# An mLSTM cell with a multiplicative FFN on one core: a chunk's own part of the outputs spread over all four quarters of TensorE

## The chip, the cores and the metric

The kernel runs on one core of one Trainium2 chip. The metric is the device time of one execution in microseconds (us). Executions of one kernel here differ by up to 4 us, and where that spread comes from is a part of the story. A "span" is the time from the first to the last instruction in the trace; it is about 1.8 us less than the device time.

## The reference

Two blocks, one after the other. The first is an mLSTM cell over 768 time steps for 4 batches of 8 heads of 40 dimensions; the second is an FFN without a nonlinearity on the 3072 tokens of 320 columns that the cell leaves. Cut to what matters:

```python
for t in range(S):
    m_new = np.maximum(f_gate[:, :, t] + m, i_gate[:, :, t])
    f_stab = np.exp(f_gate[:, :, t] + m - m_new)
    i_stab = np.exp(i_gate[:, :, t] - m_new)
    C = f_stab[..] * C + i_stab[..] * np.einsum('bhd,bhe->bhde', vt, kt)
    n = f_stab[..] * n + i_stab[..] * kt
    h_tilde = np.einsum('bhde,bhe->bhd', C, qt)
    denom = np.maximum(np.abs(nq), 1.0)
    y[:, :, t] = sigmoid(o_gate) * h_tilde / denom
...
a, b = x @ w1, x @ w2
return ((a * b) @ w3) @ w_out
```

## The kernel before

The kernel cuts time into blocks of 64 and works on two blocks of one batch at a time: a "chunk", 128 partitions, of which the lower and the upper half are the two blocks (`halves`). There are 24 chunks, numbered from 0, and one step for each. TensorE is used as four quarters of 64 rows by 64 columns: a product's row half is where its operands lie, its column half is where its output lies (`quarters`). In a full step TensorE does four groups of 16 small products, 32 instructions each, since the trace shows two for each f32 product:

- `ph`, the chunk's own part of the outputs: masked weights times values (`cell<-vbuf,pw` in the profile)
- `pi`, the part from the state before the block (`cell<-state,qT`)
- `ss`, the scores of the next chunk (`cell<-qT,kT`)
- `pc`, what the next chunk adds to the state (`cell<-vw,kbuf`)

Each step also has FFN work: the up projections (`pa`, `pb`), the down projection (`po`), early on the folding of w3 and w_out (`wp`), and late on a scheme of seven products in place of eight (`p`).

```python
halves = [slice(0, L), slice(L, P)]                 # L = 64, P = 128
quarters = ((0, 0), (1, 1), (0, 1), (1, 0))
...
ss, pc, pi = part(0, 0, L), part(0, NP * L, D1), part(1, 0, D1)
ph = [cell[1][halves[x], x, NP * D1:(NP + H) * D1]... for x in range(2)]
...
    for hd in range(H):                             # the own part: two quarters take turns
        for x, r in enumerate(halves):
            mm(ph[x][:, hd, :], pw[r, hd, :], vt[r, hd, :])
    for p in range(NP):                             # from the state: all four take turns
        for hip, x in quarters:
            mm(pi[halves[x], hip, p, :], qT[heads[hip], p, halves[x]], before[x][heads[hip], p, :])
...
# VectorE: h = pi * g, then h += ph, a half at a time
for x, r in enumerate(halves):
    nc.vector.tensor_tensor(out=h[r], in0=ph[x], in1=h[r], op=OP.add)
```

Of the kernel before, what the change touches and what calls it, by code (L numbers as in the profile page):

```python
# [11 lines left out]
OP = mybir.AluOpType  # L12
# [4 lines left out]
def kernel(  # L17
# [26 lines left out]
    nc = tc.nc  # L44

    B, H, S, D = q.shape
# [5 lines left out]
    NP = H // 2  # L52
    DP = 64
    D1 = D + 1
# [20 lines left out]
    cell = [ps_c.tile([P, 2, 512], FP, name=f"cell{i}", tag=f"cell{i}") for i in range(2)]  # L75
# [8 lines left out]
    def in_order(ins):  # L84

        if last:
            tc.add_manual_dep(ins.ins, last.pop().name, mybir.DependencyInfo(
                mybir.DependencyClass.NoSync, mybir.DependencyReason.DATA), reason="in_order")
        last.append(ins.ins)

    def mm(out, lhsT, rhs, start=True, stop=True):
        in_order(nc.tensor.matmul(out, lhsT=lhsT, rhs=rhs, start=start, stop=stop))  # L92
# [4 lines left out]
    halves = [slice(0, L), slice(L, P)]  # L97
    heads = [slice(0, D), slice(DP, DP + D)]
    quarters = ((0, 0), (1, 1), (0, 1), (1, 0))
# [207 lines left out]
    def decayed(new, old, n, x):  # L307
        c, b = divmod(n, B)
        nc.gpsimd.tensor_tensor(out=new, in0=old, op=OP.mult, in1=decay[:, b * NP:(b + 1) * NP, 2 * c + x:2 * c + x + 1]  # L309
                                .to_broadcast([P, NP, D1]))  # L310

    def quarter_work(s, rest):


        rest()

        def part(j, c0, n):
            return cell[j][:, :, c0:c0 + NP * n].rearrange("p x (n d) -> p x n d", d=n)

        ss, pc, pi = part(0, 0, L), part(0, NP * L, D1), part(1, 0, D1)  # L320
        ph = [cell[1][halves[x], x, NP * D1:(NP + H) * D1].rearrange("p (h d) -> p h d", d=D1) for x in range(2)]
        n = s - 1
        if 0 <= n < NU:
            pw, vt, qT = u_t.pop(n), vbuf[n % NB], qT_t.pop(n)
            before = before_t.pop(n)
            for hd in range(H):
                for x, r in enumerate(halves):
                    mm(ph[x][:, hd, :], pw[r, hd, :], vt[r, hd, :])
            for p in range(NP):
                for hip, x in quarters:  # L330
                    mm(pi[halves[x], hip, p, :], qT[heads[hip], p, halves[x]], before[x][heads[hip], p, :])
        n, first_read = s, None
        if n < NU:
            c, b = divmod(n, B)
            kt, vw = kbuf[n % NB], vw_t.pop(n)
            ends = range(2 if c < NT2 - 1 else 1)
            first, second, after = state[b]
            before_t[n] = first, second
            state[b] = after, second, first
            kT, qT, pw = kT_t.pop(n), qT_t[n], u_t[n]  # L340
            for p in range(NP):
                for hip, x in quarters:
                    mm(ss[halves[x], hip, p, :], kT[heads[hip], p, halves[x]], qT[heads[hip], p, halves[x]])
            for p in range(NP):
                for x, e in quarters:
                    if x in ends:
                        mm(pc[halves[e], x, p, :], kt[halves[x], 2 * p + e, :], vw[halves[x], 2 * p + e, :])
        den = None
        if 0 <= s - 1 < NU:
            den = outputs(s - 1, pi, ph)  # L350
        if n < NU:
            pv = pw.rearrange("p (n two) t -> p two n t", two=2)
            first_read = nc.vector.tensor_tensor(out=pv, in0=ss, in1=pv, op=OP.mult)
        with tc.issue_after(first_read.ins) if first_read else nullcontext():
            if n < NU:

                if c:
                    nc.vector.tensor_tensor(out=second, in0=pc[:, 0], in1=second, op=OP.add)
                else:
                    nc.vector.tensor_copy(out=second, in_=pc[:, 0])  # L360
                if len(ends) > 1:
                    decayed(after, second, n, 1)
            if den:
                done = den()
            if n < NU and len(ends) > 1:
                nc.vector.tensor_tensor(out=after, in0=pc[:, 1], in1=after, op=OP.add)
            if den:
                done = done()
        return done if den else first_read

    def outputs(n, pi, ph):
        c, b = divmod(n, B)
        hs = slice(b * H, (b + 1) * H)
        h = sb.tile([P, H, D1], FP, name="h", tag="h")
        nc.vector.tensor_tensor(out=h.rearrange("p (n two) d -> p two n d", two=2), in0=pi,
                                in1=gT[:, c, hs].rearrange("p (n two) -> p two n", two=2).unsqueeze(3)
                                .to_broadcast([P, 2, NP, D1]), op=OP.mult)
        for x, r in enumerate(halves):
            nc.vector.tensor_tensor(out=h[r], in0=ph[x], in1=h[r], op=OP.add)



        den = sb.tile([P, H, 1], FP, name="den", tag="den")

        def first():
            V = nc.vector
            V.tensor_scalar(out=den.bitcast(U32), in0=h[:, :, D:D1].bitcast(U32), scalar1=0x7FFFFFFF, scalar2=None,  # L387
                            op0=OP.bitwise_and)
            V.tensor_scalar(out=den, in0=den, scalar1=1.0, scalar2=2.0, op0=OP.max, op1=OP.mult)
            V.reciprocal(out=den, in_=den)  # L390
            return then

        def then():
            e = o_t.pop(n)
            nc.vector.scalar_tensor_tensor(out=e, in0=e, scalar=1.0, in1=den.to_broadcast([P, H, D]), op0=OP.add, op1=OP.mult)
            y_t[n] = sb.tile([P, DM + REM], FP, name="y", tag="y")
            return nc.vector.tensor_tensor(out=y_t[n][:, 0:DM].rearrange("p (h d) -> p h d", d=D), in0=h[:, :, 0:D],
                                           in1=e, op=OP.mult)

        return first  # L400
# [142 lines left out]
    for i, r in enumerate(third):  # L543
        nc.gpsimd.tensor_tensor(out=pick[r, :, i, :], in0=pair[r].to_broadcast([BH, B * NP, GC]), op=OP.mult,
                        in1=dec[r].unsqueeze(1).to_broadcast([BH, B * NP, GC]))
# [160 lines left out]
    for s in range(len(n_up)):  # L706
# [44 lines left out]
        def rest():  # L751
            for x in open_ups:
                up_rest(*x)
            if seven:
                seven[2]()

        gated = None
        if s <= NU:
            gated = quarter_work(s, rest)
        else:  # L760
            rest()
# [68 lines left out]
```

## Time and profile before

| | before |
|---|---|
| device time, median of 3 | 457.44 us (457.31 to 457.55) |
| TensorE busy | 434.4 us, 95% of the span |
| VectorE busy | 337.3 us, 74% |
| own part: products in a step | 32 instructions, from 208.19 to 208.99 us for 30 of them |
| additions of `ph` | 48 of 64x328, 497 ns each |

In the profile, PE is TensorE, PEld its weight loads, DVE VectorE, ACT ScalarE, POOL GpSimd. In a timeline a line has its start, its length, engine, line of code, operation, output and inputs, and how many instructions were merged. In the chain of waits a line has its start, its length and what took the time. A busy TensorE is not one at its peak here: by the profile products overlap (in the own part one lasts 227 ns in the median, and 30 start within 0.80 us), and a step in which it was busy throughout (15.87 us of 15.87) could still be shortened. The lines themselves stand in the prediction.

### The profile page before, as it was taken

The page shows a single profiled execution, that of the slowest core. Times are in us where ns is not written, and L with a number is a line of the kernel's source. Part 1 is how long each engine was busy: PE and PEld are TensorE (multiplying, and loading weights), DVE is VectorE, ACT ScalarE, POOL GpSimd, SP SyncE. Part 2 cuts the span into 40 slices and gives each one's busy share as a digit, 9 for nine tenths or more (in the row PEclk, how much of TensorE's full clock was granted, in tenths as well). Part 3 has the DMA queues.
Part 4 walks back from the last instruction along what each step waited for, and adds up shares of the span by engine and source line. Part 5 has one row for each costly group of instructions (what it writes and reads, how often), then busy time and mean ns, then how long its engine had stood idle before and what let it go on. Part 6 is the DMA issues. An engine that isn't in the chain of part 4 may idle for free.

```text
span 455.9 us, 12861 instructions
## 1 busy us (share of the span) xinstructions
PE 434.4 (95%) x5271; PEld 346.7 (76%) x5271; DVE 337.3 (74%) x655; ACT 134.4 (29%) x376; POOL 83.9 (18%) x156
## 2 busy tenths in 40 slices
PE   2986999999999999999999999999999999999997
PEld 2885878888778788887877877878778677777764
DVE  6689499989998988898867859659688756445530
ACT  3745355434443144133302320213210111001100
POOL 5343133233220221122022203202010000000000
PEclk9999799999999999999999999999999999999999
DMA  9989979788978788586356467274121110000001
GB/s 182 184 164 188 208 148 168 166 182 172 199 185 194 161 155 179 152 162 135 83 111 139 104 131 140 58 132 111 46 43 35 38 36 16 14 16 15 16 14 43
DMA packets 136554, 52.71 MB, mean 116 GB/s; under 512 B 109936, under 2 KB 127536, under 8 KB 136496
## 3 DMA queue, kind: packets, MB, share of 16 engines
q1 hardware_dynamic: 132896, 47.87, 52.4%
q10 hardware_dynamic: 3600, 4.03, 2.6%
q8 instruction: 41, 0.67, 0.7%
q14 instruction: 17, 0.14, 0.1%
HBM read 46.07 MB, written 5.80 MB: 114 GB/s over the span
## 4 chain that ended last, share of the span: by engine, by line
PE 80%; SPq 7%; DMA 5%; DVE 3%; issue 2%; POOL 1%; ACT 1%; DVEq 0%; ACTq 0%; POOLq 0%
PE cell L92 23%; PE pa L92 18%; PE po L92 13%; PE pb L92 11%; PE wp L92 8%; PE p L92 5%; SPq L173 3%; DMA kbuf<-in_k_dram 2%; SPq L128 1%; DMA q_all<-in_q_dram 1%; PE pt L95 1%; SPq L137 1%; PE px L95 1%; SPq L142 1%; DMA raw<-in_moe_w_out_dram 1%
## 5 line engine op out<-in xcount | busy, mean ns | idle before, releaser
L92 PE MATMUL po<-w3o,ab 128*128 128x320 f32 x224 | 62.2, 434 | 0.8 <-DVE ab L673 0.8
L92 PE MATMUL pa<-xT,w 128*128 128x256 f32 x240 | 62.2, 391 | 0.6 <-ACT xT L437 0.6
L92 PEld LDWEIGHTS po<-w3o,ab 128*128 128x128 f32 x224 | 42.3, 190 | 18.3 <-DVE ab L673 1.3
L309 POOL TENSOR_TENSOR state<-state,decay 128x164 f32<-128x164 f32 x40 | 19.8, 494 | 187.1 <-DVE den L387 161.8
L92 PEld LDWEIGHTS pa<-xT,w 128*128 128x128 f32 x240 | 45.7, 195 | 8.6 <-ACT xT L437 1.0
L630 DVE SCALAR_TENSOR_TENSOR a_sb<-pa,wo 128x512 f32<-128x512 f32 x12 | 8.3, 692 | 51.3 <-PE pa L92 51.3
L92 PE MATMUL pb<-xT,w 128*128 128x256 f32 x192 | 45.8, 382 | 0.0
L282 POOL TENSOR_SCALAR_AFFINE_SELECT pw<-pw 64x512 f32<-64x512 f32 x48 | 35.0, 728 | 54.3 <-ACT pw L280 52.8
L92 PE MATMUL cell<-w3o,ab 128*128 128x320 f32 x160 | 44.0, 432 | 0.0
L280 ACT ACTIVATE pw<-pw,aT 128x64 f32<-128x64 f32 x160 | 40.3, 336 | 2.9 <-ACT o_sb L685 2.4
L92 PEld LDWEIGHTS pb<-xT,w 128*128 128x128 f32 x192 | 37.0, 193 | 5.2
L92 PEld LDWEIGHTS cell<-w3o,ab 128*128 128x128 f32 x160 | 30.4, 190 | 12.0
L582 ACT ACTIVATE a_sb<-pa 128x512 f32<-128x512 f32 x24 | 14.3, 598 | 79.2 <-PE pb L92 79.2
L92 PE MATMUL pa<-xT,wr 64*64 64x256 f32 x384 | 36.8, 386 | 0.0
L92 PE MATMUL pb<-xT,wr 64*64 64x256 f32 x384 | 36.2, 379 | 0.0
L92 PE MATMUL wp<-wo,w3T 128*128 128x320 f32 x128 | 35.9, 433 | 0.2 <-DVE ab L583 0.2
L92 PEld LDWEIGHTS wp<-wo,w3T 128*128 128x128 f32 x128 | 23.7, 190 | 9.3 <-DVE ab L583 0.4
L92 PEld LDWEIGHTS pa<-xT,wr 64*64 64x64 f32 x384 | 19.0, 132 | 14.4 <-issue 8.4
L92 PEld LDWEIGHTS cell<-vbuf,pw 64*64 64x64 f32 x768 | 26.7, 138 | 4.2 <-issue 0.8
L583 DVE TENSOR_TENSOR ab<-pb,a_sb 128x512 f32<-128x512 f32 x24 | 16.4, 688 | 17.2 <-ACT a_sb L582 17.2
L92 PE MATMUL cell<-vbuf,pw 64*64 64x41 f32 x768 | 26.9, 229 | 0.0
L685 ACT COPY o_sb<-po 128x320 f32<-128x320 f32 x14 | 6.0, 426 | 68.9 <-PE po L92 68.9
(124 smaller groups left out, 761.6 us busy)
## 6 DMA issues: line engine op xcount, KB each, us to landing
raw<-in_moe_w_dram SPq DMA_DIRECT2D x64, 128.0 KB, 3.1
pw<-U_d SPq DMA_DIRECT2D x40, 128.0 KB, 3.9
kbuf<-in_k_dram SPq DMA_DIRECT2D x24, 160.0 KB, 4.6
vbuf<-in_v_dram SPq DMA_DIRECT2D x24, 160.0 KB, 4.9
o_in<-in_o_gate_dram SPq DMA_DIRECT2D x24, 160.0 KB, 4.4
out_dram<-o_sb ACTq DMA_DIRECT2D x24, 160.0 KB, 1.8
raw<-in_moe_w_dram SPq DMA_DIRECT2D x7, 512.0 KB, 5.9
raw<-in_moe_w_out_dram SPq DMA_DIRECT2D x32, 80.0 KB, 2.3
```

Of the source, the lines that this page charges most:

```text
L92: in_order(nc.tensor.matmul(out, lhsT=lhsT, rhs=rhs, start=start, stop=stop))
L95: in_order(nc.tensor.transpose(out, in_, ident[0:n, 0:n]))
L128: nc.sync.dma_start(out=dst, in_=rows(src, n))
L137: nc.sync.dma_start(out=dst[p0:p0 + 32, c0:c0 + NP * RAW].rearrange("r (p e) -> r p e", p=NP), in_=of.rearrange("p (r f) d -> r p (f d)", ...
L173: nc.sync.dma_start(out=dst, in_=src)
L280: nc.scalar.activation(out=pw[:, h, :], in_=src[:, h, :], func=AF.Exp, bias=aT[:, c, b * H + h:b * H + h + 1])
L282: nc.gpsimd.affine_select(out=pw[r], in_=pw[r], compare_op=OP.is_ge, fill=0.0, base=0, pattern=[[0, H], [1, L]], channel_multiplier=-1)
L309: nc.gpsimd.tensor_tensor(out=new, in0=old, op=OP.mult, in1=decay[:, b * NP:(b + 1) * NP, 2 * c + x:2 * c + x + 1] .to_broadcast([P, NP, D1]))
L582: nc.scalar.mul(out=a_sb, in_=pa, mul=UP ** -2)
L583: nc.vector.tensor_tensor(out=ab_t[gr][j][:, fs[0]:fs[-1] + 1, t0:t0 + a_sb.shape[-1]], in0=pb, in1=a_sb, op=OP.mult)
L630: nc.vector.scalar_tensor_tensor(out=out, in0=p, scalar=UP ** -2, in1=q, op0=OP.mult, op1=OP.add)
L685: nc.scalar.copy(out=o_sb, in_=po)
```

## The change

The intent is to let all four quarters take turns in the own part, as in the other three groups. Half of the products (the last four heads) write to the other column half, that is, to the other half of PSUM's partitions. `h` keeps each block in its own half of the partitions, so for these products VectorE has to read PSUM in one half and add into the other half of `h`: four additions of half the columns in place of two.

```diff
-        ph = [cell[1][halves[x], x, NP * D1:(NP + H) * D1].rearrange(...) for x in range(2)]
+        ph = [cell[1][:, x, NP * D1:2 * NP * D1].rearrange(...) for x in range(2)]
...
-            for hd in range(H):
-                for x, r in enumerate(halves):
-                    mm(ph[x][:, hd, :], pw[r, hd, :], vt[r, hd, :])
+            for hd in range(H // 2):
+                for x, e in quarters:
+                    hq = hd if x == e else hd + H // 2
+                    mm(ph[x][halves[e], hd, :], pw[halves[x], hq, :], vt[halves[x], hq, :])
...
-        for x, r in enumerate(halves):
-            nc.vector.tensor_tensor(out=h[r], in0=ph[x], in1=h[r], op=OP.add)
+        for x, e in quarters:
+            part = h[halves[x], 0:H // 2] if x == e else h[halves[x], H // 2:H]
+            nc.vector.tensor_tensor(out=part, in0=ph[x][halves[e]], in1=part, op=OP.add)
```

More of the change, by code (lines that the diff above doesn't have):

```diff
@@ L320, in quarter_work @@
         ss, pc, pi = part(0, 0, L), part(0, NP * L, D1), part(1, 0, D1)
-        ph = [cell[1][halves[x], x, NP * D1:(NP + H) * D1].rearrange("p (h d) -> p h d", d=D1) for x in range(2)]
+        ph = [cell[1][:, x, NP * D1:2 * NP * D1].rearrange("p (h d) -> p h d", d=D1) for x in range(2)]
         n = s - 1
```

## The prediction

> **What bounds the kernel now.** I read the page first (busy shares, the 40 slices), then the chain of waits in order of time, then the timeline of one step, and last a table of windows.
>
> ```profile
> PE 434.4 (95%) x5271; PEld 346.7 (76%) x5271; DVE 337.3 (74%) x655; ACT 134.4 (29%) x376; POOL 83.9 (18%) x156
> ...
> PE   2986999999999999999999999999999999999997
> ...
> DVE  6689499989998988898867859659688756445530
> ```
>
> TensorE is at 9 or above in nearly every slice, and the page's chain that ended last puts 80% of the span on it. VectorE is at 8 or 9 in about half of the slices, so it has little room early. The chain in order of time has two regimes. From 115.6 us to 357.1 us it stays on TensorE almost without a break. Before that it moves about: from 79 to 115 us it runs through the issue queue of the loads, transfers of raw weights and VectorE's conversion of them.
>
> The change is about the chunk's own part of the outputs (weights times values). One step of the TensorE timeline:
>
> ```profile
> 208.19 1.02 PE L92 MATMUL cell<-vbuf,pw 64*64 64x41 f32 x30
> 208.99 0.26 PE L92 MATMUL cell<-state,qT 40*64 40x41 f32 x2
> 209.04 0.23 PE L92 MATMUL cell<-vbuf,pw 64*64 64x41 f32 x2
> 209.07 0.61 PE L92 MATMUL cell<-state,qT 40*64 40x41 f32 x28
> 209.48 0.25 PE L92 MATMUL cell<-qT,kT 40*64 40x64 f32 x2
> ...
> 210.01 0.66 PE L92 MATMUL cell<-vw,kbuf 64*64 64x41 f32 x31
> 210.60 0.55 PE L95 MATMUL px<-ident,y 128*128 128x128 f32 x3
> ```
>
> Each of the four groups is 32 instructions (16 products in source, two instructions each in f32). The own part holds TensorE from 208.19 to 208.99 for 30 instructions: 26.7 ns each. The other three groups already go round all four quarters. The last of them, `cell<-vw,kbuf`, has exactly the shape that the own part will have (64x41, 64*64): 31 starts within 0.66 - 0.23 us (the length of one), so 0.43 us over 30 steps: 14.4 ns each. The reader is to see that equal work runs at almost half the cost where four quarters take turns.
>
> [...] The new code keeps row half x in bank x, as the other groups do, so nothing new has to wait there. [...] the two 64-partition additions take 1.01 us together at 497 ns each, with no overlap, whereas the 128-partition instructions behind them overlap (0.69 us long, the next starting 0.61 us later).
>
> **The change, part by part.**
>
> On TensorE nothing is removed or added: the 32 instructions of a chunk keep their shape and change their order and places. Per chunk 32 x 26.7 ns = 0.85 us becomes 32 x 14.4 ns = 0.46 us: 0.39 us less, 24 chunks. The order of all other instructions on every engine is the same in both builds; on VectorE only the two additions become four.
>
> VectorE replaces 2 additions of 64x328 by 4 of 64x164. The groups of instructions:
>
> ```profile
> L379 DVE TENSOR_TENSOR h<-cell,h 64x328 f32<-64x328 f32 x48 | 23.9, 497 | 1.1
> ...
> L358 DVE TENSOR_TENSOR state<-cell,state 128x164 f32<-128x164 f32 x20 | 6.4, 318 | 0.0
> ```
>
> The cost goes by columns, not partitions, so an addition with 164 columns should cost about the 318 ns of `state<-cell,state`[...]. All four alternate between the halves of their output, so none should overlap: 4 x (326 + 16) = 1.37 us against 2 x 513 = 1.03 us (16 ns is the gap that the pair shows). That is 0.34 us more per chunk, 8 us more of busy VectorE in all. Where it counts is a question of stage.
>
> Stage A, 115 us to the last step. The own part starts 14 times in it, from 128.79 to 342.08 us.
>
> ```profile
> 72.00:88.00 16.00, 16.00 (x289) 13.45 (x289) 14.92 (x33) 7.42 (x21) 3.50 (x6) 1.00 0.81 168
> 192.50:208.37 15.87, 15.87 (x219) 12.93 (x216) 13.63 (x26) 5.39 (x15) 3.32 (x6) 1.00 0.82 159
> ```
>
> (Columns: window, length, then busy time and count of TensorE, its weight loads, VectorE, ScalarE, GpSimd; then clock, DMA share, GB/s.) The second row is one step of this stage: TensorE idles 0 of 15.87 us, VectorE is busy 13.63. With the change the step is 15.48 us and VectorE 13.97, still 1.5 us short. Most of its idle time is one wait of 1.54 us for ScalarE's copy of the up product, which absorbs the addition. I looked for waits of TensorE that could become real. The product that follows the cell block (`wp`, at 210.99 us) needs a bank that VectorE frees by 209.74; it will come at 210.6, so 0.9 us remain. From 251 us on, the seven-product scheme writes the banks that the additions read: at 342 us the additions end at 345.64 and the bank is written at 347.17, a margin of 1.5 us; TensorE comes 0.39 earlier and the additions end 0.34 later, so some 0.8 us remain. So all is kept: 14 x 0.39 = 5.5 us.
>
> Stage B, the last step. Here VectorE is on the path:
>
> ```profile
> 357.64 0.81 DVE ab L628 x2
> 358.84 0.50 DVE h L375
> 359.36 0.49 DVE h L379
> 359.86 0.52 DVE h L379
> 360.51 2.83 PE p L92 x12
> ```
>
> TensorE waits 1.10 us for the additions because the banks change owner there. VectorE is busy with `ab` while the own part runs, so its 0.39 us buy nothing, and the additions cost 0.34 us: -0.34 us.
>
> Stage C, before 115 us, 9 own parts. The chain touches the cell block at 23.2, 36.4, 53.2 and 62.5 us; the first runs at about twice the cost (1.83 us for 30, where the others take 1.02), so up to 0.8 + 3 x 0.39 = 2.0 us could come. But then it turns to transfers (4 to 9 us each from one wait), and from 56 to 120 us VectorE is busy 14.3 to 15.3 of each 16 us. The first row above is such a window. There the added 0.34 us of the five chunks from 62 to 112 us push the conversion of weights, whose result TensorE awaits at 115.6 us: up to -1.7 us. I take the two as cancelling: 0, give or take 1.5 us.
>
> Sum: 5.5 - 0.34 + 0 = 5.2 us. 457.4 - 5.2 = 452.3 us, 1.1% less.
>
> **The rivals.**
>
> (1) [...] some wait of the new order spoils it: nothing is gained on TensorE and VectorE's extra stays: 457.4 + 0.3 to 2, so up to 459.5 us. Against it are three groups in the same banks that run at 14 ns. Unlikely.
>
> (2) VectorE becomes the bound in stage A as well. Its 13.97 us against 15.48 speak against it, and the waits followed above. If the additions across halves were much slower than within a half (say by double: 1.4 us more per chunk), it would just fill the step, stage B and C would lose some 8 us, and the result would be near 459 us. No instruction in the trace before reads PSUM in one half and writes SBUF in the other, so this is the part that I can't measure beforehand.
>
> (3) All 24 own parts count: 23 x 0.39 + 0.4 extra for the slow first one - 0.34 = 9.0 us, 448.4 us, 2.0% less. Against it: before 115 us the chain is mostly elsewhere[...].
>
> (4) Stage C loses its full 1.7 us and gains none: 454.0 us.
>
> **Range and chances.** Stage A is measured on both sides, so its 5.5 us should hold within 0.7; stage C adds 1.5 either way; a little more is left on the low side for rival 3 and on the high side for slow additions. That gives 450.0 to 454.6 us. Over 2% faster needs below 448.3 us, beyond even rival 3 as worked out: 3%. Over 2% slower needs 466.6 us, which no rival reaches: 1%. Within 2%: 96%.
>
> **What would show it.** The timeline: the own part's 32 instructions start within about 0.46 us and the next group follows; steps between 128 and 224 us last 15.5 in place of 15.88 us. The groups: four additions per chunk, x96, about 326 ns; VectorE's busy time near 345 us. The start of `wp` near 115.6 us: earlier or later tells stage C by itself. The wait of `p` for `h`: near 1.1 + 0.34 us, or more as TensorE comes earlier. The prediction is wrong if the own part stays above 20 ns each, if the additions exceed 400 ns, or if the place where the chain settles on TensorE moves by over 2 us.

## The result, and the profile after

The changed kernel took 453.15 us (median of 4, 451.65 to 453.54), the kernel before in the same rounds 457.5 us (457.31 to 458.13). The ratio is 0.9897, with a 95% interval of 0.9871 to 0.9922. A ratio here is the mean time of one kernel's fast runs over that of the other's of the same rounds, so it is not quite the ratio of the medians. In class terms this is "same": about 1% faster, inside of 2%. The predicted 452.3 us was off by 0.85 us, and the measured time lies in the range.

The page of the changed kernel, to be held against the first fence and the addition's line in the prediction:

```profile
PE 428.3 (95%) x5271; PEld 339.4 (75%) x5271; DVE 342.5 (76%) x703; ACT 134.5 (30%) x376; POOL 84.1 (19%) x156
...
L382 DVE TENSOR_TENSOR h<-cell,h 64x164 f32<-64x164 f32 x96 | 31.2, 325 | 1.8
```

TensorE is busy for 6.1 us less with the same 5271 products. There are 96 additions in place of 48, at 325 ns. Their busy time went from 23.9 to 31.2 us. All 96 took 319 to 332 ns, within a half or across, so reading PSUM in one half and writing the other cost nothing extra here.

The timeline of TensorE in one step, the one that starts its own part at 208.19 us before:

```profile
205.80 0.62 PE L92 MATMUL cell<-vbuf,pw 64*64 64x41 f32 x32
206.24 0.66 PE L92 MATMUL cell<-state,qT 40*64 40x41 f32 x32
206.71 0.67 PE L92 MATMUL cell<-qT,kT 40*64 40x64 f32 x32
207.20 0.63 PE L92 MATMUL cell<-vw,kbuf 64*64 64x41 f32 x32
207.76 0.55 PE L95 MATMUL px<-ident,y 128*128 128x128 f32 x3
```

The reader is to see the starts: the own part holds TensorE from 205.80 to 206.24, 0.44 us, and is now like its three neighbours. From its start to the transposition behind the four groups (`px`) are 1.96 us, before 2.41 (208.19 to 210.60): 0.45 us less.

The table of windows of the changed kernel, one stretch before and one step after 128 us (columns as in the prediction):

```profile
72.00:88.00 16.00, 15.68 (x353) 13.12 (x347) 15.02 (x35) 8.66 (x26) 3.49 (x6) 1.00 0.82 157
190.38:205.80 15.42, 15.42 (x215) 12.52 (x211) 13.82 (x28) 5.38 (x15) 3.31 (x6) 1.00 0.82 163
```

In the second line TensorE is still busy for the whole step, which is now 15.42 us long and not 15.87, and VectorE, at 13.82, has 1.6 us left. In the first line TensorE has idle time, where it had none.

The last step, VectorE's timeline and then the waits of TensorE from 340 us on:

```profile
351.77 0.68 DVE L631 TENSOR_TENSOR ab<-pb,wo 128x512 f32<-128x512 f32 x1
352.37 0.49 DVE L377 TENSOR_TENSOR h<-cell,gT 128x328 f32<-128x328 f32 x1
352.89 1.34 DVE L382 TENSOR_TENSOR h<-cell,h 64x164 f32<-64x164 f32 x4
```

```profile
PE p L92 <- DVE h L382: 1.9, 1, 1.9
```

The same wait in the kernel before:

```profile
PE p L92 <- DVE h L379: 1.1, 1, 1.1
```

The four additions take 1.34 us where the two took 1.01, and TensorE waits 1.9 us for them, before 1.1 us. The 0.8 us more are the sum of two things: TensorE comes 0.45 us earlier, and the additions end 0.34 us later.

To see where the 6.1 us of span between the two profiles went, I cut each trace by the starts of the own parts, read off TensorE's timeline. C is the time to the start of the tenth own part, A from there to the start of the last (the 24th), B from there to the end:

| | C | A | B | span |
|---|---|---|---|---|
| before | 128.79 | 228.01 | 99.14 | 455.94 |
| changed | 128.67 | 221.66 | 99.49 | 449.82 |

A is shorter by 6.35 us, which is 14 x 0.454. B is longer by 0.35 us. C is the same in these two profiles, although nine own parts lie in it.

### The profile page after: what moved, and what is told of

Its sections match the earlier page's. It is cut to its first block, busy times and chain, and to the rows that moved or that the text cites. A ratio compares the mean times of both kernels' runs of the same rounds, so it can differ in the third digit from the quotient of the medians.

```text
span 449.8 us, 12909 instructions
## 1 busy us (share of the span) xinstructions
PE 428.3 (95%) x5271; PEld 339.4 (75%) x5271; DVE 342.5 (76%) x703; ACT 134.5 (30%) x376; POOL 84.1 (19%) x156
## 4 chain that ended last, share of the span: by engine, by line
PE 75%; DMA 8%; SPq 8%; DVE 4%; issue 2%; ACT 1%; POOL 0%; DVEq 0%; ACTq 0%
PE cell L92 21%; PE pa L92 16%; PE po L92 13%; PE pb L92 10%; PE wp L92 7%; PE p L92 5%; SPq L173 4%; DMA kbuf<-in_k_dram 3%; DMA raw<-in_moe_w_dram 2%; DMA raw<-in_moe_w_out_dram 2%; SPq L128 2%; DMA q_all<-in_q_dram 1%; PE pt L95 1%; SPq L137 1%; PE px L95 1%
## 5 line engine op out<-in xcount | busy, mean ns | idle before, releaser
L382 DVE TENSOR_TENSOR h<-cell,h 64x164 f32<-64x164 f32 x96 | 31.2, 325 | 1.8
L178 ACT ACTIVATE raw<-raw 128x512 f32<-128x512 f32 (+1 forms) x32 | 19.1, 627 | 12.4 <-DMA raw<-in_moe_w_dram 11.2
```

The lines of the kernel that those rows point to most:

```text
L178: nc.scalar.activation(out=hi, in_=hi, func=AF.Prelu, scale=2.0 ** -111, alpha=2.0 ** 32)
L382: nc.vector.tensor_tensor(out=part, in0=ph[x][halves[e]], in1=part, op=OP.add)
```

## The experiments

Ten runs followed, all correct (again is the changed kernel once more, the others are new kernels). In all of them A and B came out the same to 0.02 us wherever the own part and the additions were the same, so I take one profile to settle them. C did not, and it is what makes single executions differ. For timed runs, which have no trace, I take C as the run's span less the A and B of the kernel's profile; errors in brackets after a mean are standard errors.

### again: the changed kernel once more

No edit.

> The changed kernel once more, for its spread. Its four runs lay between 451.65 and 453.54 us and its profile, the fastest of them, showed stage A (first own part of the PE-bound steps to the last own part) shorter by 6.3 us, the last stage longer by 0.36 us and the stretch before 128 us shorter by only 0.1 us. Theory: steps of 15.43 us again, own part of 32 products within 0.45 us, and the spread of the time comes whole from the stretch before 128 us: the start of the tenth own part moves by 1 to 2 us between this profile and the last, the rest to within 0.2 us. Rival: the spread comes from the TensorE clock or from stage A; then steps differ between the two profiles. Time 451.5 to 454 us.

It took 453.35 us (450.75 to 453.9, five runs) beside 457.9 us for the kernel before; ratio 0.9884 (0.9855 to 0.9913). Its profile has A at 221.66 and B at 99.48, as in the first profile of the changed kernel, and C at 130.96, not 128.67. So the theory holds: the spread lies in C. With the first four runs, nine runs of the changed kernel have a mean C of 129.9 us (0.4); all 35 runs of the kernel before have 129.0 us (0.1).

The rival, TensorE's clock, falls for A and B but not for C. The granted clock averages 0.95 over C in the first profile of the changed kernel and 0.92 in this one, and 1.00 from there to the end in both. It does not order the profiles by itself (C is 131.60 us at 0.96 in adds_alone and 128.36 us at 0.91 in last_step_old), so the cause of the spread stays open.

### pairs: the same places, two quarters at a time

```diff
-            for hd in range(H // 2):
-                for x, e in quarters:
+            for pair in (quarters[:2], quarters[2:]):
+                for hd in range(H // 2):
+                    for x, e in pair:
```

> Same places for the outputs and the same four additions, but only two quarters take turns at a time (first the two of the first heads, then the two of the last heads). Theory [...]: back to about 26.7 ns an instruction, 0.85 us per own part, steps of 15.87 us, and the time is that of before plus the additions: 457.8 to 459.6 us. Rival (the new places of the outputs, both halves of both banks, bring the gain): 14 ns an instruction, 453 us.

456.52 us (ratio 0.9965, 0.9936 to 0.9993). Both expectations missed: A is 225.21 us, 3.55 more than in the changed kernel and 2.80 less than before, and a step is 15.68 us. TensorE's timeline of one own part:

```profile
175.85 0.70 PE L92 MATMUL cell<-vbuf,pw 64*64 64x41 f32 x26
176.33 0.25 PE L92 MATMUL cell<-state,qT 40*64 40x41 f32 x2
176.38 0.23 PE L92 MATMUL cell<-vbuf,pw 64*64 64x41 f32 x2
176.41 0.23 PE L92 MATMUL cell<-state,qT 40*64 40x41 f32 x2
176.44 0.23 PE L92 MATMUL cell<-vbuf,pw 64*64 64x41 f32 x2
```

The group behind the own part starts while six instructions of the own part, three in each of two quarters, have not started, though it was issued after them. The single starts in the trace show the same inside the own part: in one quarter they follow each other at 58 ns (176.202, 176.260, 176.318 us), and the first of the second pair starts at 176.064 us, while six instructions of the first pair, again three in each quarter, are still to come. So what counts here is how long each quarter's own row of instructions is, not only how many quarters take turns in the order of issue. A row of eight at 58 ns is 0.47 us. Two rows one after the other would be 0.93 us, but the second starts while three instructions of the first are left. The rival that the new places bring the gain falls: places and additions are those of the changed kernel, and more than half of the gain in A is gone.

### rowpairs: two quarters that share a row half

```diff
-            for hd in range(H // 2):
-                for x, e in quarters:
+            for x in range(2):
+                for hd in range(H // 2):
+                    for e in (x, 1 - x):
```

> As pairs (two quarters at a time), but the two that take turns share a row half and differ in the output half. Theory: each quarter takes one instruction per 58 ns by itself, whichever the other one is, and the engine runs a few products ahead into a free quarter: as in pairs, steps of 15.68 us between 144 and 220 us. Rival [...]: the own part takes 32 x 58 ns = 1.9 us where the changed kernel takes 0.45, steps near 16.8 us.

One run (too few for a state), 455.34 us. A is 225.04 us and a step 15.69 us, as the theory has it; in pairs they are 225.21 and 15.68 us. So it makes no difference here which two quarters take turns. The rival falls: the 32 instructions of one own part start within 0.65 us (191.77 to 192.42 us), not 1.9.

### serial: one quarter after the other

```diff
-            for hd in range(H // 2):
-                for x, e in quarters:
+            for quarter in quarters:
+                for hd in range(H // 2):
+                    for x, e in [quarter]:
```

> The same 32 instructions one quarter after the other, eight in each. pairs came out between both theories (steps of 15.68 us), since the second pair of quarters started when some six products of the first were still outstanding. Theory (each quarter in its own order, with a look ahead of some six products): about two quarters at work at a time, own part near 1.05 us, steps near 16.0 us. Rival (products start strictly in program order): 32 x 58 ns = 1.87 us, steps near 16.8 us. If the look ahead were the whole queue: 15.43 us as in the changed kernel.

One run (too few for a state), 461.08 us. TensorE's timeline of one own part and its neighbours:

```profile
192.88 1.21 PE L92 MATMUL cell<-vbuf,pw 64*64 64x41 f32 x29
193.87 0.26 PE L92 MATMUL cell<-state,qT 40*64 40x41 f32 x3
...
194.04 0.23 PE L92 MATMUL cell<-vbuf,pw 64*64 64x41 f32 x1
```

From the first to the last start are 1.16 us, where 31 gaps of 58 ns would be 1.80 us in strict order and the changed kernel takes 0.40. A step is 16.19 us, nearer to the 16.0 expected than to 16.8. So starts run ahead of the order of issue here, and not over the whole queue. It is not by the six products that I expected: the four quarters start at 192.882, 193.091, 193.351 and 193.611 us, the last three each right behind the fifth of the eight starts of the quarter before, with three left. In pairs and rowpairs six were left because two quarters had three each. So here starts run ahead by three instructions in each quarter. A is 231.66 us, 10.0 us more than in the changed kernel, by nothing but the order of the same 32 instructions in a group. And its C is 128.14 us, the shortest of all profiles: nine own parts, each 0.7 us longer or more, show no cost before the tenth. It is one execution, but if they all counted they would cost over 6 us, more than C moves by itself.

### adds_alone: the kernel before, with four additions

```diff
-        for x, r in enumerate(halves):
-            nc.vector.tensor_tensor(out=h[r], in0=ph[x], in1=h[r], op=OP.add)
+        for i in range(2):
+            hh = slice(i * H // 2, (i + 1) * H // 2)
+            for x, r in enumerate(halves):
+                nc.vector.tensor_tensor(out=h[r, hh], in0=ph[x][:, hh], in1=h[r, hh], op=OP.add)
```

> The kernel before with its two additions of 64x328 cut into four of 64x164, nothing else: the cost on VectorE alone. Theory: steps from 128 us on stay at 15.88 us (absorbed), the last stage is 0.34 us longer, and before 128 us it costs between 0 and 1.7 us: 457.8 to 459.5 us. If VectorE sets the pace before 128 us (rival a): near 459.3 us, the tenth own part starting 1.5 us later. If transfers set it (rival b): near 457.8 us.

458.55 us (ratio 1.002, 0.9995 to 1.0045). A is 228.01 us, as before to the last digit: the additions are absorbed there. B is 99.49 us, 0.35 more. The mean C of its six runs is 129.6 us (0.5), which is neither the 1.5 us of rival (a) nor clearly rival (b): 0.4 us later than before, with an error as large.

### adds_twice: eight additions

```diff
         for x, e in quarters:
-            part = h[halves[x], 0:H // 2] if x == e else h[halves[x], H // 2:H]
-            nc.vector.tensor_tensor(out=part, in0=ph[x][halves[e]], in1=part, op=OP.add)
+            for i in range(0, H // 2, H // 4):
+                h0 = i if x == e else i + H // 2
+                part = h[halves[x], h0:h0 + H // 4]
+                nc.vector.tensor_tensor(out=part, in0=ph[x][halves[e], i:i + H // 4], in1=part, op=OP.add)
```

> The changed kernel with each of its four additions cut in two (eight of 64x82): VectorE does about 8 x 257 - 4 x 341 = 0.69 us more per chunk. Theory: steps from 128 us on stay at 15.43 us (VectorE had 1.6 us to spare, 0.9 remain), the last stage is 0.69 us longer than in the changed kernel (100.2 in place of 99.5 us from the last own part to the end). Before 128 us: if VectorE sets the pace there, the tenth own part starts 3 to 6 us later than the 129.9 us that is the mean of nine runs of the changed kernel; if transfers do, within 1 us of it. Time 454 if transfers, 457 to 460 us if VectorE.

453.74 us (ratio 0.9906, 0.9892 to 0.992). VectorE's timeline:

```profile
193.93 1.62 DVE L384 TENSOR_TENSOR h<-cell,h 64x82 f32<-64x82 f32 x8
195.59 0.69 DVE L355 TENSOR_TENSOR pw<-cell,pw 128x512 f32<-128x512 f32 x1
```

The eight take 1.62 us, only 0.28 more than the four: I had given each 257 ns, the cost of one that waits for the one before, and they take 203 ns each on average. Unlike the four, they go to the same half two at a time. That such a pair overlaps is my reading; the view shows only the eight together. A stays at 221.66 us: absorbed again. B is 99.76 us, 0.27 more than in the changed kernel, so all of it is paid in the last step. The mean C of its four fast runs is 130.6 us (0.2), 0.6 later than in the changed kernel with an error of 0.4. If VectorE alone set the pace of C, 0.28 x 9 = 2.5 us would be the most; 0.6 is about a quarter of it, and within two errors anything from nothing to over a half.

### middle: the change in chunks 9 to 22 only

```diff
+            if 9 <= n < NU - 1:
                 ... the four quarters, four additions
+            else:
+                ... the old form, two additions
```

> The change only in chunks 9 to 22, whose own parts run in the PE-bound steps; the first nine chunks and the last one as in the kernel before. Theory: stage A keeps its 6.3 us, the last stage and the stretch before 128 us are as before: 457.5 - 6.3 = 451.2 us, faster than the changed kernel's median of 453.2 by up to 2 us. Rival (VectorE's extra work costs nothing outside the last step, and the changed kernel's 453.2 is its own noise): at 451.2 to 453 us, within 0.5 us of the changed kernel on the same chip.

451.95 us (450.89 to 453.86, six runs; ratio 0.9873, 0.9848 to 0.9899). A is 221.66 us and B 99.15: the whole gain of A without the cost in B. Its C, where it is the kernel before, has a mean of 129.6 us (0.5). It is 1.4 us faster than the changed kernel by the medians, but only 0.34 us of that are shown by A and B; the rest lies within what C does by itself.

### early: the change in chunks 0 to 8 only

Against middle:

```diff
-            if 9 <= n < NU - 1:
+            if n < 9:
```

> The change only in chunks 0 to 8; the others, the last one too, as in the kernel before. Theory: from the tenth own part on, as before to 0.1 us (228.0 and 99.1 us); the nine faster own parts bring nothing and the start of the tenth lies between 129 and 130.5 us in the mean: time equal to before within 1 us (457.5 to 459 us). Rival (the change gains in every chunk): 9 x 0.45 = 4 us faster, 454 us.

457.84 us (ratio 0.9989, 0.9975 to 1.0004) beside 458.25 us. A is 228.01 and B 99.15, as before. The mean C of six runs is 128.8 us (0.25), beside 129.1 us (0.15) for the kernel before on the same chip. Nine faster own parts and 18 more additions bring nothing that can be told from nothing; a gain of 4 us is ruled out.

The table of windows shows where those nine parts' time goes: the same 64 us of the kernel before and then of the changed kernel (the profile of again):

```profile
56.00:120.00 64.00, 62.47 (x997) 53.04 (x995) 59.81 (x126) 30.54 (x85) 19.16 (x33) 1.00 0.85 173
```

```profile
56.00:120.00 64.00, 59.77 (x990) 50.26 (x989) 60.55 (x135) 31.06 (x86) 17.93 (x31) 0.97 0.83 165
```

TensorE is busy for 2.7 us less and waits that much more. VectorE is busy for 93% to 95% and the DMA engines for over 80% of this stretch.

### last_step: the cell's products first in the last step

```diff
-        rest()
+        if s < NU:
+            rest()          # the remaining products of the up projection
...
             den = outputs(s - 1, pi, ph)
+        if s == NU:
+            rest()
```

> The changed kernel, with the last chunk's own part and its part from the states put ahead of the remaining products of the up projection in the last step, so that VectorE can add while TensorE works. A version that may beat both. Theory (in the last step TensorE waits 1.90 us for VectorE's additions only because VectorE is still busy with the up projection's sums): that wait goes or falls below 0.9 us; but the own part now follows the down products and must wait some 0.7 us for ScalarE to empty their bank. From the tenth own part to the end: 321.15 us in the changed kernel, 320.0 to 320.7 here; time about 452.5 us. Rival (the wait is set by the additions themselves): 321.15 us stays.

452.31 us (451.22 to 453.81, five runs; ratio 0.9872, 0.985 to 0.9893). The waits of TensorE from 340 us on:

```profile
PE p L92 <- DVE a_sb L636: 1.0, 1, 1.0
...
PE cell L92 <- ACT o_sb L691: 0.5, 1, 0.5
```

From the tenth own part to the end are 220.47 + 100.27 = 320.74 us, 0.41 less than the 321.15 of the changed kernel and 0.04 outside what I expected. The wait of 1.9 us became one of 1.0, and the bank that ScalarE has to empty costs 0.5 us: both parts of the theory show, but the gain is a little smaller.

### last_step_old: the same, with the last chunk in the old form

To last_step is added:

```diff
+            if n < NU - 1:
                 ... the four quarters, four additions
+            else:
+                ... the old form, two additions
```

> As last_step, but the last chunk in the old form (two quarters, two additions). Theory: here the own part is on TensorE's path and the additions are hidden, so that the new form is worth its 0.45 us in the last step too: 0.3 to 0.45 us longer from the tenth own part to the end than last_step. Rival (the last step is VectorE's): 0.35 us shorter.

One run (too few for a state), 450.94 us. From the tenth own part to the end are 220.47 + 100.40 = 320.87 us, 0.13 more than last_step. That is between the two expectations. TensorE's wait for VectorE is 0.7 us here and 1.0 us there, so about 0.3 of the 0.45 us that the new form saves turns into waiting: the last step is bound by both engines in turn.

None of the versions is far ahead of the changed kernel. By A and B, last_step (320.74), middle (320.81) and last_step_old (320.87) beat it (321.15) by 0.3 to 0.4 us, less than C moves from one execution to the next. All four are some 6 us ahead of the kernel before (327.15).

## Why the prediction was right or wrong

**Direction and size.** Right: predicted -5.2 us, measured -4.4 us by the medians of the first rounds. Over nine runs of the changed kernel and all 35 of the kernel before, the mean times differ by 5.1 us (A and B give -6.0, C +0.9). That the sum came so close is in part luck: A gained 0.9 us more than predicted, and C lost about as much where 0 was predicted.

**What bounds the own part.** The reading of the timeline (equal work at almost half the cost where four quarters take turns) was right in what follows from it and loose in one size. I took 26.7 ns for an instruction by dividing 0.80 us by 30. Those 30 contain the start of the group, where the first starts of a quarter follow at 36 and 51 ns, and the 0.80 us end where the next group has already started ahead of the last two. In the steady state every second start in the trace before lies 58 ns apart (192.401, 192.459, 192.518, 192.576 us), and in the other three groups every fourth start does, so one quarter's rate is the same in all four, with 41 or 64 columns streamed and 40 or 64 rows. So in this trace it is one instruction per 58 ns and quarter, 29 ns for one where two take turns. There were 16 of them in a quarter before, and there are 8 now. 8 x 58 ns = 0.47 us is what can be saved, and 0.45 us is what was; I had 0.39 us. Over 14 steps the term is 6.35 and not 5.5 us, which is more than the 0.7 us that I allowed for it. That it is the taking of turns and not the places is shown by pairs, rowpairs and serial, which have the same places and lose 3.4 to 10.0 us in A. What the 58 ns consist of was not shown: no run changed that number.

**The additions.** 326 ns each were predicted, an estimate of mine, and 325 measured; four take 1.34 us, predicted 1.37. From the trace before alone, 497 ns at 328 columns and 692 ns at 512 (`pw<-cell,pw`) give an estimate of 323 ns for 164. There the cost goes by columns: 494 ns with 128 partitions (`h<-cell,gT`) and 497 with 64, both of 328 columns. The prediction's worry about adding across halves fell. VectorE's whole busy time rose by 5.2 us and not by the predicted 8: the additions' own rose by 7.3 (the 8 counts the gaps between them), and other instructions took less.

**Stage A absorbs them.** Right, by adds_alone (A the same to 0.01 us) and by adds_twice. No wait of TensorE appeared in that stage.

**Stage B.** Right: -0.34 us predicted, -0.35 measured, in every kernel with four additions in the last chunk, and gone in middle and early, which have two there. last_step shows that the additions count there because VectorE reaches them late.

**Stage C.** Predicted 0, give or take 1.5 us. Nine runs beside 35 say 0.9 us lost with an error of 0.4, and the five of last_step, with the same first nine chunks, 1.1 beside the runs of their rounds (0.5). But early, which has these nine chunks too, says 0.4 gained (0.3). These don't agree within their errors, so whether the change costs up to 1 us in C stays open. That the nine faster parts don't bring their 4 us is shown by early, and serial fits. That transfers rather than VectorE set the pace there was only in part shown: adds_twice puts VectorE's share at about a quarter of its extra time (0.6 us of 2.5, error 0.4). In the first profile of the changed kernel the chain of waits came to TensorE like this:

```profile
117.40 4.64 DMA raw<-in_moe_w_dram
122.25 0.49 issue
122.73 0.46 ACT xT L440
123.24 1.99 PE pa L92 x8
```

It settles on TensorE at 123.2 us, before at 115.6. I had named a move of over 2 us as a sign that the prediction fails. It moved and yet the tenth own part started 0.1 us earlier. What moved it was not shown. In the profile of again, the same kernel, the chain is on TensorE from 107 us on, and there the tenth own part starts 2.3 us later. So the place where a chain settles was a bad sign to name; the start of a fixed piece of work is a good one. What makes C take between 127.9 and 131.7 us in six runs of one and the same kernel (pairs) stays open.

**The rivals.** Number 1 (nothing gained) and number 2 (VectorE becomes the bound) fell with A. Number 3 (all 24 count) fell with early. Number 4 (C loses its full 1.7 us) is not what the mean shows: 0.9 us, about two errors from 1.7 and from 0.

## What to carry to other kernels

For groups of small products like these, count the instructions that each quarter of TensorE gets and multiply by what one quarter takes for one (58 ns here). Where all four quarters took turns in the order of issue, that was about the time of the group (8 x 58 ns = 0.47 us, 0.44 in the timeline). The same 32 instructions in the same places gave steps of 15.42 us with four quarters in turn, 15.68 to 15.69 us with two, and 16.19 us one quarter after another. Spreading over idle quarters gained 6.35 us in the stage where TensorE was the bound and VectorE had 1.6 us to spare, even though VectorE had to add across halves. Take such a rate from the middle of a group (58 ns here), not from its ends (36 and 51 ns at the start). Price an engine's extra work stage by stage: here 0.34 us per chunk on VectorE were free in the 14 chunks of stage A, could not be told from C's own spread in the first nine, and were paid in full in the last one, where TensorE waits for them.
